# A layer kernel whose last four token tiles are transposed in 32x32 blocks on VectorE, by way of DRAM, and whose first weight rows are loaded one by one

## The chip, the cores and the metric

The kernel runs on one core of one Trainium2 chip. The metric is the device time of one execution in microseconds (us). Other work does not share the core. The engines are TensorE (PE in the profile; its weight loads are PEld), VectorE (DVE), ScalarE (ACT), GpSimd (POOL) and SyncE (SP). SP computes nothing here: it is the queue on which nearly all DMA transfers are issued, in the order of the program.

## The reference

The input `x` has 2048 tokens of 512 numbers. After a layer norm, two branches read the same normalized rows, and the output is `x + s * g`:

```python
xn = _layernorm(x, axis=-1)
s = _A_ref(xn, A_wqkv, A_w_phi, A_wo)                 # linear attention, 32 heads of 16
g = _silu(_B_ref(xn, B_W_gate, B_W_up, B_W_down))     # gated ReLU unit, 1376 wide
return x + s * g
...
qkv = (x @ wqkv) ...                                  # q, k, v
phi_k = concat(softmax(k @ w_phi), softmax(-(k @ w_phi)))       # and phi_q alike
o = phi_q (phi_k^T v) / (phi_q (phi_k^T 1) + 1e-6);  s = o @ wo
h = relu(x @ W_gate) * (x @ W_up);  g = silu(h @ W_down)
```

Everything is float32. The kernel keeps that precision by splitting each operand into a high part and a low part (`split`, L193) and making each product from three matmuls (`mm3`, L198).

## The kernel before, in words

**Stage 1, tokens.** The 2048 tokens are 16 tiles of 128 rows, and the loop `for n in range(N)` (L1046) takes one tile in each turn. Loads, norms and transposes run ahead of it: a turn `n` loads tile n+7 (`load_x`), takes the sums of tile n+6 on ScalarE (`norm_stats`), the inverse root of tile n+5 on VectorE and GpSimd (`norm_scale`), applies the norm of tile n+4 on ScalarE (`norm_apply`), and transposes tile n+3 (`turn`, LEAD = 3). `turn` (L320) is four TensorE transposes of 128x128 into one PSUM bank, `pxT` (`transpose_x`); then ScalarE writes the high part into the SBUF tensor `XT` (`hi_xt`) and a full copy `xf` (`full_xt`), and VectorE writes the low part (`lo_xt`), both from PSUM. From each two neighbouring tiles GpSimd makes four sums and differences (`sums_x`, into new tiles `sa` and `sb`), which `sums_hi` (ScalarE) and `sums_lo` (GpSimd) split into `XT` too. For the first eight tiles most of `XT` is spilled to DRAM and read back for the second half of stage 2.

In the same turn TensorE projects tile n to keys (`pk`, 12 matmuls of 512 columns) and values (`pv`, 12), one of sixteen query pieces (`pq`, 12), and adds phi^T v of an earlier tile to four PSUM banks that stay occupied through the stage (`pkv`, 8 matmuls of 256 columns). VectorE makes the exponents from `pk` (two reductions, two subtractions), later the low part of v, the sums, a reciprocal that it writes into the bank of `pv`, and the scaled features `ek`. The pool of PSUM banks has 8; with four held by `pkv`, four go round.

**Stage 2, gated unit and queries.** For each half of the tokens and each of 11 slices of the hidden width, `gate_up` makes seven products (`pa` to `pd`) and `down` adds rows of `py`. Beside that runs the query side (`all_queries`, `q_pair`): VectorE turns the stored query pieces back in 32x32 blocks, finds bounds, ScalarE exponentiates, and so on. Between `state()` (L1119), which builds the attention state, and the first query pair of the first half stands `yield 24,` (L1176).

**What sets the order.** Instructions keep the order of the program on each engine. That order comes from a planner, the class `Clock` (L62): it counts columns of TensorE work (`now`; a matmul of 512 columns adds 542), estimates when each tile will be ready (a DMA 8000 after its issue), and at every `pump()` releases the next step of generators whose wants are met: for the wants "sync" and "tensor" 3000 counts after the estimate, for an engine when its backlog is under a limit. `yield k,` waits k times 512 counts. Nothing of this exists at run time; there, each engine waits for semaphores, in order.

**Start.** Before the loop, the weights of keys, queries and values are loaded on SP in the order written in L960 to L991, folded on TensorE (`fold`) and split; `wv_hi` and `wv_lo` (L977, L980) split the value rows k = 0 to 3 on ScalarE and GpSimd.

Of the kernel before, what the change touches and what calls it, by code (L numbers as in the profile page):

```python
# [1 line left out]

# [5 lines left out]
F32 = mybir.dt.float32  # L8
F32R = mybir.dt.float32r
AF = mybir.ActivationFunctionType  # L10
# [28 lines left out]
START = (12, 15)  # L39
WO_WITH = (4, 5, 6, 7)  # L40

A21, A22, A11, A12, S1, S2, S3, S4 = range(8)


class InOrder:
# [16 lines left out]
class Clock:  # L62
# [4 lines left out]
    LIMIT = {"vector": 2000, "scalar": 2000, "gpsimd": 2500}  # L67
    MARGIN = 3000
    LANDING, ISSUE = 8000, 1500
    shared = None  # L70

    def __init__(self):
        self.free = dict.fromkeys(self.FIXED, 0.0)
# [10 lines left out]
    def issued(self, key, name, a, k):  # L84
        o, ins = a[0], [*a[1:], *k.values()]
        n = max(x.free_size() for x in [o, *ins] if hasattr(x, "free_size"))
        start = max([self.now, *(self.there(x) + 200 for x in ins)])
        if name == "dma_start":
            self.ready[o.name] = start + self.LANDING
            if key == "gpsimd":  # L90
                self.free[key] = max(start, self.free[key]) + self.ISSUE
            return
        cost = self.RATE[key] * n
        if key == "tensor":
            n = o.free_size()
# [6 lines left out]
        self.ready[o.name] = self.free[key] + (380 if key == "tensor" else 0)  # L102

    def add(self, gen, after=0, limit=1, first=False):
        self.work.insert(0 if first else len(self.work), [self.now + after * BT, (None,), gen, limit])
# [53 lines left out]
def layer_kernel(ctx: ExitStack, tc: tile.TileContext, x, wkT, wqT, wv, wo, wf, cst, out):  # L159
# [24 lines left out]
    def f32(t):  # L184
        return t.bitcast(F32)

    def add(engine, o, a, b, op=ALU.add):
        engine.tensor_tensor(o, a, b, op=op)
# [62 lines left out]
        return lambda: split(*map(by_parity, w[k]), even_first(p))  # L251


    mhalf = sb.tile([P, 96], F32, name="mhalf")[:, 0:1]
    XT = sb.tile([P, 8, 2, 2, BT], F32R, tag="XT", name="XT")
    pace.shared = XT.name
    XN, XF, SF = {}, {}, {}

    def norm_stats(n):
        xt = X.pop(n)  # L260
        xn = u2((P, D), "xn")
        sm, ss, rs, bias = small(1, "lm"), small(1, "lv"), small(1, "lr"), small(1, "lb")
        nc.scalar.activation(xn, xt, AF.Copy, scale=-1.0 / D, accum_out=sm)
        nc.scalar.activation(xn, xt, AF.Square, bias=sm, accum_out=ss)
        XN[n] = xn, xt, bias, rs, sm, ss

    def norm_scale(n):
        xn, xt, bias, rs, sm, ss = XN[n]
        nc.vector.tensor_scalar(rs, ss, 1.0 / D, 1e-5, op0=ALU.mult, op1=ALU.add)
        nc.gpsimd.tensor_tensor(rs, rs, mhalf, op=ALU.pow)  # L270

    def norm_apply(n):
        xn, xt, bias, rs, sm, ss = XN[n]
        nc.vector.tensor_scalar(bias, sm, rs, None, op0=ALU.mult)
        nc.scalar.activation(xn, xt, AF.Identity, bias=bias, scale=rs)
        XN[n] = xn

    def norm_vector(n):

# [14 lines left out]
    def cols(n):  # L294
        i = order[n][1]
        return slice(i * P, (i + 1) * P)
# [8 lines left out]
    def xt_part(n, s):  # L305

        a = A21 if n % 2 else A11
        return XT[:, a:a + 2, s, :, cols(n)]

    def hi_xt(n, p):  # L310
        nc.scalar.activation(xt_part(n, 0), p, AF.Copy)

    def full_xt(n, p):
        XF[n] = u2((P, 2, 2, P), "xf")
        nc.scalar.activation(XF[n], p, AF.Copy)

    def lo_xt(n, p):
        add(nc.vector, xt_part(n, 1), p, f32(xt_part(n, 0)), ALU.subtract)

    def turn(m, full=True):  # L320
        p = transpose_x(m)
# [5 lines left out]
    def sums_x(n):  # L327

        x0, x1 = XF.pop(n - 1), XF.pop(n)
        sa, sb_ = u2((P, 2, 2, P), "sa"), u2((P, 2, 2, P), "sb")  # L330
        add(nc.gpsimd, sa[:, 0], x1[:, 0], x1[:, 1])
        add(nc.gpsimd, sb_[:, 0], x0[:, 0], x1[:, 0], ALU.subtract)
        add(nc.gpsimd, sa[:, 1], sa[:, 0], x0[:, 0], ALU.subtract)
        add(nc.gpsimd, sb_[:, 1], x0[:, 1], sa[:, 1], ALU.subtract)
        SF[n] = sa, sb_

    def sums_hi(n):
        for s, c in zip(SF[n], (S1, S3)):
            nc.scalar.activation(XT[:, c:c + 2, 0, :, cols(n)], s, AF.Copy)

    def sums_lo(n):
        for s, c in zip(SF.pop(n), (S1, S3)):
            add(nc.gpsimd, XT[:, c:c + 2, 1, :, cols(n)], s, f32(XT[:, c:c + 2, 0, :, cols(n)]), ALU.subtract)

    def xt_cols(n):
        a, c = A21 if n % 2 else A11, cols(n)
# [107 lines left out]
    DONE = set()  # L454

    def f_load(f):
        if f == AHEAD[-1]:

            t = u4((P, 2, 2, 2, P), "rawg")
            RAW[f] = [t[:, c] for c in range(2)], u2((P, D), "rawd")  # L460
            nc.sync.dma_start(t.rearrange("p c k s f -> p (c k s f)"), wf[f][:, :1024])
        else:
            RAW[f] = two("rawg", f not in AHEAD), u2((P, D), "rawd")
            for c in range(2):
                nc.sync.dma_start(RAW[f][0][c].rearrange("p k s f -> p (k s f)"), wf[f][:, c * 512:(c + 1) * 512])
        nc.sync.dma_start(RAW[f][1], wf[f][:, 1024:])

    def w_pair(name):
# [556 lines left out]
    folds[1]()  # L1025
    norm_vector_apply(3)

    def all_preps():
# [16 lines left out]
    at = [0]  # L1045
# [287 lines left out]
```

## Time and profile before

| | us |
|---|---|
| three runs | 562.86, 564.63, 564.69 (median 564.63) |
| profiled execution, device time | 562.9 |
| its span, first to last instruction | 561.1 |
| outside the span | 1.8 |
| mean granted TensorE clock | 0.999 |

The span is read on the timeline of the engines. Stage 1 turns take 8.7 to 9.8 us each and end at 166.9 us; the first half of stage 2 ends at about 355 us with the last `pso` matmuls, and the second half takes the rest. In the views, tile names stand for the operands, L58 is the line of the helper through which every instruction is recorded, and times are from the start of the span. In the chain of waits each row is start, length and group.

### The profile page before, as it was taken

Reading aid. Unit: us, or ns where it says so; the run is one execution under the profiler, and the core shown is the slowest. Engines: PE = TensorE matmul, PEld = TensorE weight load, DVE = VectorE, ACT = ScalarE, POOL = GpSimd, SP = SyncE. Lnnn points to the kernel's source line nnn. Section 1 sums busy time; section 2 is a strip of 40 time slices with the busy share of each in tenths; the row PEclk is TensorE's granted clock in tenths of the full one; section 3 lists DMA queues with packets and bytes.
Section 4 is the critical chain, followed back from the end, with each engine's and each line's share of the span. In section 5 each row is a group of like instructions: output and inputs, shape, how many; then the busy total and the mean of one; then the engine's idle time right before and its main releaser. Section 6 shows DMA issues by size and latency. Waiting matters only on the chain.

```text
span 561.1 us, 8204 instructions
## 1 busy us (share of the span) xinstructions
PE 556.3 (99%) x2618; PEld 466.0 (83%) x2618; DVE 412.0 (73%) x623; ACT 282.7 (50%) x504; POOL 416.2 (74%) x356
## 2 busy tenths in 40 slices
PE   9999999999999999999999999999999999999997
PEld 8888888888888888888888888888888888888886
DVE  5978777677656898999798432699995959775324
ACT  3898687765545456444425251234463544534500
POOL 1689987898888386998889242572879788888474
PEclk9999999999999999999999999999999999999999
DMA  8349999765599827979767899997475666659675
GB/s 282 136 150 245 274 277 330 213 167 166 150 297 314 327 77 276 326 270 324 263 240 230 246 356 419 401 374 282 137 225 178 219 204 206 207 166 284 170 237 193
DMA packets 84538, 137.98 MB, mean 246 GB/s; under 512 B 7824, under 2 KB 34320, under 8 KB 83600
## 3 DMA queue, kind: packets, MB, share of 16 engines
q1 hardware_dynamic: 81040, 125.33, 65.1%
q0 software_dynamic: 3312, 12.06, 11.0%
q8 instruction: 21, 0.34, 0.3%
q14 instruction: 21, 0.17, 0.1%
q10 hardware_dynamic: 144, 0.07, 0.0%
HBM read 76.87 MB, written 52.69 MB: 231 GB/s over the span
## 4 chain that ended last, share of the span: by engine, by line
PE 99%; DVE 0%; issue 0%
PE py L58 21%; PE pc L58 11%; PE pa L58 11%; PE pd L58 11%; PE pv L58 8%; PE pk L58 8%; PE pq L58 8%; PE pso L58 8%; PE pb L58 5%; PE pkv L58 3%; PE pnum L58 3%; PE pxT L58 1%; PE pfold L58 1%; PE pidle L58 1%; PE pz L58 0%; DVE yk L58 0%
## 5 line engine op out<-in xcount | busy, mean ns | idle before, releaser
L58 PE MATMUL py<-fdh,hl 128*128 128x512 f32 x176 | 68.5, 389 | 0.0
L58 PE MATMUL py<-fdh,hh 128*128 128x512 f32 x176 | 68.5, 389 | 0.0
L58 PE MATMUL py<-fdl,hh 128*128 128x512 f32 x176 | 68.5, 389 | 0.0
L58 PE MATMUL pa<-XT,wa 128*128 128x512 f32 x264 | 67.4, 389 | 0.0
L58 POOL TENSOR_TENSOR hl<-e,hh 128x512 fp32r<-128x512 f32 x22 | 28.5, 1296 | 44.9 <-ACT hh L58 40.0
L58 PEld LDWEIGHTS pa<-XT,wa 128*128 128x128 f32 x264 | 49.5, 188 | 10.2
L58 ACT ACTIVATE hh<-e 128x512 fp32r<-128x512 f32 x22 | 13.9, 633 | 72.5 <-DVE e L58 70.1
L58 DVE TENSOR_TENSOR y<-py,y 128x512 f32<-128x512 f32 x40 | 27.5, 689 | 24.7 <-PE py L58 24.7
L58 POOL TENSOR_TENSOR phl<-ek,phl 128x1024 fp32r<-128x1024 f32 x15 | 36.1, 2409 | 11.1 <-ACT phl L58 11.1
L58 PE MATMUL pv<-wvh,XT 128*128 128x512 f32 x128 | 43.5, 401 | 0.0
L58 PE MATMUL pk<-wkh,XT 128*128 128x512 f32 x128 | 42.4, 392 | 0.0
L58 POOL TENSOR_TENSOR hl<-u,hh 128x512 fp32r<-128x512 f32 x22 | 28.8, 1311 | 16.6 <-ACT hh L58 14.3
L58 POOL TENSOR_TENSOR ez<-eq,zB 128x1024 f32<-128x1024 f32 x16 | 38.5, 2411 | 3.3 <-ACT eq L58 2.7
L58 PE MATMUL pq<-XT,wqh 128*128 128x512 f32 (+1 forms) x144 | 40.3, 366 | 0.0
L58 PEld LDWEIGHTS py<-fdh,hl 128*128 128x128 f32 x176 | 33.0, 188 | 6.9
L58 PEld LDWEIGHTS py<-fdh,hh 128*128 128x128 f32 x176 | 33.0, 188 | 6.8
L58 PEld LDWEIGHTS py<-fdl,hh 128*128 128x128 f32 x176 | 33.0, 188 | 6.8
L58 POOL TENSOR_TENSOR ol<-of,oh 128x512 fp32r<-128x512 f32 (+1 forms) x13 | 19.9, 1551 | 23.3 <-ACT oh L58 15.9
L58 PE MATMUL pc<-XT,wc 128*128 128x512 f32 x132 | 34.9, 392 | 0.0
L58 PE MATMUL pd<-XT,wc 128*128 128x512 f32 x132 | 33.8, 389 | 0.0
L58 PE MATMUL pc<-XT,wb 128*128 128x512 f32 x132 | 33.7, 389 | 0.0
L58 PE MATMUL pd<-XT,wd 128*128 128x512 f32 x132 | 33.5, 389 | 0.0
(162 smaller groups left out, 1581.0 us busy)
## 6 DMA issues: line engine op xcount, KB each, us to landing
zacc<-ek POOLq DMA_DIRECT2D x15, 512.0 KB, 6.0
xts<-XT SPq DMA_DIRECT2D x4, 1792.0 KB, 8.8
XT<-xts SPq DMA_DIRECT2D x7, 1024.0 KB, 19.6
wa<-ws SPq DMA_DIRECT2D x26, 256.0 KB, 5.0
wb<-ws SPq DMA_DIRECT2D x26, 256.0 KB, 4.4
wc<-ws SPq DMA_DIRECT2D x26, 256.0 KB, 5.0
ws<-wa SPq DMA_DIRECT2D x22, 256.0 KB, 4.5
ws<-wb SPq DMA_DIRECT2D x22, 256.0 KB, 4.2
```

Source lines behind the costliest of these rows:

```text
L58: return self.tc.keep_in_program_order(op(*a, **k))
```

## The change

Four things are changed.

1. Tiles 12 to 15 (`BLOCKWISE = 12`) are no longer transposed on TensorE. `norm_apply` writes them with columns regrouped, and a generator `by_blocks` stores the tile to DRAM, loads it back in four transfers that spread 32-row blocks over the partitions (runs of 128 numbers, 512 bytes), transposes it on VectorE in 32x32 blocks, and makes the high and low parts from the result in SBUF, without a PSUM bank and without the full copy. (`pace.mark("scalar")` is a name that stands for the planner's present estimate of ScalarE; `hi_xt` and `lo_xt` regroup their views of `XT` to the blocks.) Loads, sums, scales and norms of the last tiles are drawn one turn ahead (`up_to`).
2. `sums_x` works in place in `xf`, for all tiles; the order of the combinations in `XT` changes to match.
3. At the start, value rows 0 to 3 and query rows 2 and 3 are loaded in a transfer each, instead of two rows in one; the second prefetched gate slice is loaded in two transfers instead of one.
4. The `yield 24,` before the first query pair is gone.

```diff
-A21, A22, A11, A12, S1, S2, S3, S4 = range(8)
+A21, A22, A11, A12, S3, S1, S2, S4 = range(8)
+BLOCKWISE = 12
+LAND = (12, 12)
...
     def norm_apply(n):
...
+        if n < BLOCKWISE:
+            nc.scalar.activation(xn, xt, AF.Identity, bias=bias, scale=rs)
+        else:
+            nc.scalar.activation(xn.rearrange("p (a k i) -> p k a i", a=4, i=32),
+                                 xt.rearrange("p (k a i) -> p k a i", a=4, i=32), AF.Identity, bias=bias, scale=rs)
+            TURN[n] = pace.add(by_blocks(n, xn), 0, 3, True)
+
+    def by_blocks(n, xn):
+        xd = dram((P, D), f"xn{n}")
+        yield "sync", xn
+        nc.sync.dma_start(xd, xn)
+        yield LAND[0],
+        yield "sync", xd
+        t = u2((P, 4, P), "xp")
+        for a in range(4):
+            r = slice(32 * a, 32 * a + 32)
+            nc.sync.dma_start(t[r], xd.rearrange("(b q) (a c) -> a q b c", q=32, a=4)[a])
+        yield LAND[1],
+        yield "sync", t
+        while at[0] < n - LEAD:
+            yield 1,
+        yield "vector", t
+        o = u2((P, D), "xf")
+        nc.vector.transpose(o, t.rearrange("p b c -> p (b c)"))
+        XF[n] = o.rearrange("p (b c k q) -> p c k b q", b=4, c=2, k=2)
+        yield "scalar", o
+        hi_xt(n, XF[n])
+        yield "vector", pace.mark("scalar")
+        lo_xt(n, XF[n])
+        if n % 2:
+            yield "gpsimd", o
+            sums_x(n)
...
     def sums_x(n):
-        sa, sb_ = u2((P, 2, 2, P), "sa"), u2((P, 2, 2, P), "sb")
-        add(nc.gpsimd, sa[:, 0], x1[:, 0], x1[:, 1])
...
+        add(nc.gpsimd, x1[:, 1], x1[:, 0], x1[:, 1])
+        add(nc.gpsimd, x1[:, 0], x0[:, 0], x1[:, 0], ALU.subtract)
+        add(nc.gpsimd, x0[:, 0], x1[:, 1], x0[:, 0], ALU.subtract)
+        add(nc.gpsimd, x0[:, 1], x0[:, 1], x0[:, 0], ALU.subtract)
...
-    nc.sync.dma_start(wv_raw[:, 0:2, :], wv[:, 0:2, :])
-    nc.sync.dma_start(wq_raw[:, 2:4, :], wqT[:, 2:4, :])
+    for k in range(2):
+        nc.sync.dma_start(wv_raw[:, k, :], wv[:, k, :])
+    for k in range(2, 4):
+        nc.sync.dma_start(wq_raw[:, k, :], wqT[:, k, :])
     load_x(2)
-    nc.sync.dma_start(wv_raw[:, 2:4, :], wv[:, 2:4, :])
+    for k in range(2, 4):
+        nc.sync.dma_start(wv_raw[:, k, :], wv[:, k, :])
...
-        if n + 7 < N:
-            load_x(n + 7)
+        up_to(n + 7 + (n > 6), load_x)
...
-        if 1 < n < N - 4:
-            norm_apply(n + 4)
-        if 0 < n < N - 5:
-            norm_scale(n + 5)
+        if n > 1:
+            up_to(n + 4 + (n > 9), norm_apply)
+        if n:
+            up_to(n + 5 + (n > 8), norm_scale)
...
-        turned = [turn(n + LEAD)] if 1 < n < N - LEAD else [turn(3)] if n == 1 else []
+        if 1 < n < N - LEAD and m >= BLOCKWISE:
+            turned = []
+        else:
+            turned = [turn(m)] if 1 < n < N - LEAD else [turn(3)] if n == 1 else []
...
-        if n + 6 < N:
-            norm_stats(n + 6)
+        up_to(n + 6 + (n > 7), norm_stats)
         if n % 2 and n + 2 < N:
+            for m in (n + 1, n + 2):
+                if m in TURN:
+                    pace.finish(TURN.pop(m))
             sums_hi(n + 2)
...
             yield from state()
-            yield 24,
```

More of the change, by code (lines that the diff above doesn't have):

```diff
@@ L1 @@
 from contextlib import ExitStack
+from types import SimpleNamespace
 import concourse.bass as bass
@@ L69 @@
     LANDING, ISSUE = 8000, 1500
-    shared = None
+    shared, marks = None, 0
     def __init__(self):
@@ L102, in issued, with mark @@
         self.ready[o.name] = self.free[key] + (380 if key == "tensor" else 0)
+    def mark(self, key):
+        self.marks += 1
+        t = SimpleNamespace(name=f"mark{self.marks}")
+        self.ready[t.name] = self.free[key]
+        return t
     def add(self, gen, after=0, limit=1, first=False):
@@ L251, in fold @@
         return lambda: split(*map(by_parity, w[k]), even_first(p))
-    mhalf = sb.tile([P, 96], F32, name="mhalf")[:, 0:1]
+    mhalf = sb.tile([P, 96], F32, name="mhalf")
+    mhalf, eps = mhalf[:, 0:1], mhalf[:, 1:2]
     XT = sb.tile([P, 8, 2, 2, BT], F32R, tag="XT", name="XT")
     pace.shared = XT.name
-    XN, XF, SF = {}, {}, {}
+    XN, XF, SF, TURN, at = {}, {}, {}, {}, [0]
     def norm_stats(n):
@@ L261, in norm_stats @@
         xn = u2((P, D), "xn")
+        unread = xn or ps(name="unread")
         sm, ss, rs, bias = small(1, "lm"), small(1, "lv"), small(1, "lr"), small(1, "lb")
-        nc.scalar.activation(xn, xt, AF.Copy, scale=-1.0 / D, accum_out=sm)
-        nc.scalar.activation(xn, xt, AF.Square, bias=sm, accum_out=ss)
-        XN[n] = xn, xt, bias, rs, sm, ss
+        nc.scalar.activation(unread, xt, AF.Copy, scale=-1.0 / D, accum_out=sm)
+        nc.scalar.activation(unread, xt, AF.Square, bias=sm, accum_out=ss)
+        XN[n] = xt, bias, rs, sm, ss, xn
     def norm_scale(n):
-        xn, xt, bias, rs, sm, ss = XN[n]
+        xt, bias, rs, sm, ss, xn = XN[n]
         nc.vector.tensor_scalar(rs, ss, 1.0 / D, 1e-5, op0=ALU.mult, op1=ALU.add)
@@ L272, in norm_apply @@
     def norm_apply(n):
-        xn, xt, bias, rs, sm, ss = XN[n]
+        xt, bias, rs, sm, ss, xn = XN[n]
         nc.vector.tensor_scalar(bias, sm, rs, None, op0=ALU.mult)
-        nc.scalar.activation(xn, xt, AF.Identity, bias=bias, scale=rs)
-        XN[n] = xn
+        xn = xn or u2((P, D), "xn")
+        if n < BLOCKWISE:
+            nc.scalar.activation(xn, xt, AF.Identity, bias=bias, scale=rs)
+            XN[n] = xn
+        else:
[27 more added lines that the diff above has]
+            sums_x(n)
     def norm_vector(n):
@@ L308, in xt_part, with like @@
         return XT[:, a:a + 2, s, :, cols(n)]
+    def like(t, p):
+        return t.rearrange("p c k (b q) -> p c k b q", q=32) if len(p.shape) == 5 else t
     def hi_xt(n, p):
-        nc.scalar.activation(xt_part(n, 0), p, AF.Copy)
+        nc.scalar.activation(like(xt_part(n, 0), p), p, AF.Copy)
     def full_xt(n, p):
@@ L317, in lo_xt @@
     def lo_xt(n, p):
-        add(nc.vector, xt_part(n, 1), p, f32(xt_part(n, 0)), ALU.subtract)
+        add(nc.vector, like(xt_part(n, 1), p), p, f32(like(xt_part(n, 0), p)), ALU.subtract)
     def turn(m, full=True):
@@ L329, in sums_x @@
         x0, x1 = XF.pop(n - 1), XF.pop(n)
-        sa, sb_ = u2((P, 2, 2, P), "sa"), u2((P, 2, 2, P), "sb")
-        add(nc.gpsimd, sa[:, 0], x1[:, 0], x1[:, 1])
[L332 to L335, printed above, removed]
+        add(nc.gpsimd, x1[:, 1], x1[:, 0], x1[:, 1])
+        add(nc.gpsimd, x1[:, 0], x0[:, 0], x1[:, 0], ALU.subtract)
+        add(nc.gpsimd, x0[:, 0], x1[:, 1], x0[:, 0], ALU.subtract)
+        add(nc.gpsimd, x0[:, 1], x0[:, 1], x0[:, 0], ALU.subtract)
+        SF[n] = x1, x0
     def sums_hi(n):
-        for s, c in zip(SF[n], (S1, S3)):
-            nc.scalar.activation(XT[:, c:c + 2, 0, :, cols(n)], s, AF.Copy)
+        for s, c in zip(SF[n], (S3, S2)):
+            nc.scalar.activation(like(XT[:, c:c + 2, 0, :, cols(n)], s), s, AF.Copy)
     def sums_lo(n):
-        for s, c in zip(SF.pop(n), (S1, S3)):
-            add(nc.gpsimd, XT[:, c:c + 2, 1, :, cols(n)], s, f32(XT[:, c:c + 2, 0, :, cols(n)]), ALU.subtract)
+        for s, c in zip(SF.pop(n), (S3, S2)):
+            add(nc.gpsimd, like(XT[:, c:c + 2, 1, :, cols(n)], s), s, f32(like(XT[:, c:c + 2, 0, :, cols(n)], s)),
+                ALU.subtract)
     def xt_cols(n):
@@ L456, in f_load @@
     def f_load(f):
[L457 to L465, printed above, removed]
+        RAW[f] = two("rawg", f not in AHEAD), u2((P, D), "rawd")
+        for c in range(2):
+            nc.sync.dma_start(RAW[f][0][c].rearrange("p k s f -> p (k s f)"), wf[f][:, c * 512:(c + 1) * 512])
         nc.sync.dma_start(RAW[f][1], wf[f][:, 1024:])
@@ L1026, in layer_kernel, with up_to @@
     norm_vector_apply(3)
+    done = {norm_scale: 5, norm_apply: 5, norm_stats: 5, load_x: 6}
+    def up_to(m, op):
+        for i in range(done[op] + 1, min(m, N - 1) + 1):
+            op(i)
+            done[op] = i
     def all_preps():
@@ L1060, in layer_kernel @@
             pace.pump()
-        turned = [turn(n + LEAD)] if 1 < n < N - LEAD else [turn(3)] if n == 1 else []
+        m = n + LEAD
+        if 1 < n < N - LEAD and m >= BLOCKWISE:
+            turned = []
+        else:
+            turned = [turn(m)] if 1 < n < N - LEAD else [turn(3)] if n == 1 else []
         pace.pump()
```

1 line of the change is left out of this document (removed).

## The prediction, made before the result was seen

> **What bounds the kernel now.** I read the page's busy shares first, then the waits of TensorE, then the windows, because a share alone does not say whether an engine waits.
>
> ```profile
> PE 556.3 (99%) x2618; PEld 466.0 (83%) x2618; DVE 412.0 (73%) x623; ACT 282.7 (50%) x504; POOL 416.2 (74%) x356
> ```
> ```profile
> PE pidle L58 <- DVE mhalf L58: 1.1, 1, 1.1
> ```
> ```profile
> 0.00:10.00 10.00, 8.94 (x54) 8.78 (x55) 3.82 (x11) 3.30 (x5) 0.77 (x5) 1.00 0.79 245
> 520.00:561.00 41.00, 37.40 (x181) 31.43 (x179) 13.51 (x20) 9.50 (x18) 23.17 (x19) 0.99 0.66 200
> ```
>
> The second fence is the whole list of waits of TensorE: one, of 1.1 us, at the start. The windows (columns: PE, PEld, DVE, ACT, POOL, clock, DMA share, GB/s) show where the 4.8 us that are not PE lie: 1.06 before its first instruction and 3.6 after its last. Between them TensorE has work without a break, at full clock. So time goes only when TensorE has fewer instructions, and is lost only when something makes it wait. All else in the change counts through that second door. The bound for "no change" is 0.5% either way, 2.8 us, about what a measurement of this kernel can tell from none.
>
> **Part 1, the transposes removed.** The chain of waits in order of time shows one turn with a transposed tile and one without:
>
> ```profile
> 115.69 2.72 PE pk L58 x12
> 118.41 0.95 PE pkv L58 x8
> 119.36 0.44 PE pxT L58 x4
> 119.80 2.76 PE pv L58 x12
> 122.55 2.72 PE pq L58 x12
> ...
> 134.86 2.72 PE pk L58 x12
> 137.58 0.95 PE pkv L58 x8
> 138.53 2.75 PE pv L58 x12
> 141.28 2.72 PE pq L58 x12
> ```
> ```profile
> 115.69:125.27 9.58, 9.58 (x49) 8.14 (x49) 8.02 (x12) 5.49 (x9) 9.50 (x10) 1.00 0.74 201
> 125.27:134.86 9.59, 9.59 (x50) 8.15 (x49) 6.72 (x10) 5.39 (x9) 9.11 (x9) 1.00 0.81 210
> 134.86:144.00 9.14, 9.14 (x45) 7.71 (x45) 6.13 (x9) 4.65 (x8) 8.01 (x10) 1.00 0.45 117
> ```
>
> The same pk, pkv, pv and pq stand in both; the turn is 9.59 with four pxT and 9.14 without, 0.45 us. Four tiles (12 to 15, in turns 9 to 12): 4 x 0.45 = **1.8 us off the bound**. That is the only TensorE work that changes.
>
> **Part 2, what the new path adds, and where it lies.**
>
> ```profile
> L58 DVE STREAM_TRANSPOSE pq<-pql 128x512 f32<-128x512 f32 x16 | 11.3, 704 | 0.0
> L58 DVE TENSOR_TENSOR XT<-pxT,XT 128x512 fp32r<-128x512 f32 x16 | 11.0, 690 | 6.9 <-ACT xf L58 5.4 <-ACT XT L58 1.5
> L58 DVE TENSOR_TENSOR yk<-yk,sx 128x512 f32<-128x512 f32 x1 | 1.3, 1254 | 0.0
> ```
> ```profile
> L58 ACT ACTIVATE xf<-pxT 128x512 f32<-128x512 f32 x16 | 9.4, 588 | 0.0
> ```
>
> VectorE gains four block transposes of this very shape, 4 x 0.70 = 2.8 us. Its low part now has both operands in SBUF: 0.69 if that is free, 1.25 by the one row of that kind, so 0 to 0.56 more per tile. Together 0.7 to 1.3 us per turn, on a busy time of 6.7 and 8.0 in the two turns quoted: under 9.3 even in the fuller one, whose neighbours have room. ScalarE loses the full copy, 0.59 per tile. GpSimd does the same sums, in place. None of this is on TensorE, so it is costed at nothing; the cover is the slack below.
>
> The Trainium skill, "SBUF — State Buffer", section "SBUF: two separate sides", says that a VectorE instruction with two SBUF inputs and a GpSimd one that reads SBUF exclude each other for a whole instruction. The 1254 ns against 690 agree with it; by that rule each low part could also hold a GpSimd instruction up, and the four of them would cost VectorE 2.2 us, still off TensorE.
>
> The wait added is VectorE's: the transpose stands in its queue until the four loads have landed. Behind it stand the exponents of the turn, the features, and so the release of the PSUM banks.
>
> ```profile
> 91.21 0.80 ACT L58 ACTIVATE xn<-xt,lb,lr 128x512 f32<-128x512 f32 x1
> 99.43 0.80 ACT L58 ACTIVATE xn<-xt,lb,lr 128x512 f32<-128x512 f32 x1
> 111.78 0.80 ACT L58 ACTIVATE xn<-xt,lb,lr 128x512 f32<-128x512 f32 x1
> ```
> ```profile
> 87.81 2.75 PE pk L58 x12
> ...
> 106.10 2.72 PE pk L58 x12
> ```
> ```profile
> 117.34 1.22 DVE L58 TENSOR_TENSOR ek<-ek,pv 128x1024 f32<-128x1024 f32 x1
> ```
> ```profile
> 110.14 0.41 SPq L58 DMA_DIRECT2D ws<-wa  x1
> 110.64 0.41 SPq L58 DMA_DIRECT2D ws<-wb  x1
> ```
> ```profile
> pq<-pqs SPq DMA_DIRECT2D x12, 128.0 KB, 2.8
> ws<-wd SPq DMA_DIRECT2D x1, 256.0 KB, 2.8
> ```
> ```profile
> xt<-x SPq DMA_DIRECT2D x16, 256.0 KB, 7.3
> ```
>
> Tiles 12, 13 and 14 are normed at 91.2, 99.4 and 111.8 (turns 8, 9, 10). After that come the store, four issues of 0.41, and the landing of the loads. From the landings between 88 and 140 us: 2.8 + 1.6 + 2.8 = 7.2 us; from the median of the x loads (most of them in the crowded start): 7.3 + 1.6 + 7.3 = 16.2. I take 7.2, since those rows are of the same stage and queue, and keep 16.2 for the range. The planner lets the transpose into VectorE's queue about 10.5 us after the start of the turn in which the tile is normed: 3000 counts of margin, then twice 8000 + 3000, and 542 counts are one matmul of 2.72/12 = 0.227 us, so 1.3 + 2 x 4.6. The turns start with pk; for tile 12 that is 87.8 + 10.5 = 98.3, for tile 14 106.1 + 10.5 = 116.6, where VectorE is busy with turn 10's features (ek, to 118.6). Data are there at 92.0 + 7.2 = 99.2 and 112.6 + 7.2 = 119.8. So VectorE stands 1 to 2 us per tile, less for 13, nothing for 15, which must wait for turn 12 anyway. The twenty extra SP issues (4 tiles x 5 x 0.41 = 8 us over 40) and 2 MB move nothing that TensorE reads in this stage.
>
> The slack: four banks go round, and without pxT a turn asks for three. The last reader of turn 10's pv is the ek above; it ends at 118.6, and its bank is next asked for at turn 11's pq, 122.1 without the transposes: 3.5 us, against one request earlier (119.8) before. A stand of 1 to 2 us is hidden; I put 0.3 us into the sum for small losses.
>
> **Part 3, start and queries.**
>
> ```profile
> 16.05 1.15 ACT L58 ACTIVATE wvh<-wvr 128x512 fp32r<-128x512 f32 x2
> 16.75 2.56 POOL L58 TENSOR_TENSOR wvl<-wvr,wvh 128x512 fp32r<-128x512 f32 x2 [1.01 <-ACT wvh L58]
> ```
> ```profile
> 17.50 2.76 PE pv L58 x12
> ```
>
> TensorE has no wait at the start, so single rows cannot gain anything. They can lose: the low part of the last value row ends at 19.31, and the last of the four groups of pv begins at 17.50 + 3/4 x 2.76 = 19.6. Cover 0.3 us. But ScalarE starts on rows 2 and 3 without waiting for a DMA, so the three extra issues (3 x 0.41 = 1.2 us on SP) must first eat the time by which the rows are early. Value 0, bounds 0 and +0.9 (1.2 less the cover).
>
> ```profile
> 186.53 0.72 DVE L58 STREAM_TRANSPOSE pq<-pql 128x512 f32<-128x512 f32 x1
> ```
> ```profile
> 180.00:195.00 15.00, 15.00 (x68) 12.43 (x67) 11.96 (x20) 7.14 (x15) 7.58 (x5) 1.00 0.93 344
> 195.00:210.00 15.00, 15.00 (x68) 12.43 (x67) 14.83 (x22) 7.57 (x14) 11.12 (x11) 1.00 0.22 80
> ```
>
> `yield 24,` is 24 x 512 counts, 5.1 us: the first query pair moves from 186.5 to about 181.4, into a window where VectorE has 3 us free. TensorE stayed at 15.00 of 15 even where VectorE was at 14.83, so I cost this at 0, bounds -0.5 and +1. The in-place sums and the split gate load: 0.
>
> **Sum.** -1.8 + 0.3 = -1.5 us: 562.9 becomes 561.4. The median of the three runs is 1.7 above the profiled execution, and the four times stand at two levels, 562.9 and 564.6; from the upper one the same step gives 563.1. I predict 562.3, between, 0.3% down on either.
>
> **Rivals.**
>
> *The gain comes back as waits* (562.3 + 1.8, about 564). Several small losses of the bounds above, a late bank here, a late row there, add up to the 1.8. For it: GpSimd at 9.50 of 9.58 in turn 11, so whatever blocks it shifts the low parts. Against: features are used three turns later.
>
> *VectorE waits for DRAM and TensorE for VectorE* (slower). Place: turns 9 to 11, at the new transpose. It decides where store, issues and loads take more than about 9.5 us: tile 14's data must be there by 118.6 + 3.5 of slack, from 112.6. Each us beyond that is a us of TensorE, for tiles 12, 13 and 14. Halfway between the two prices (11.7 us), 3 x 2.2 = 6.6 us less the 1.8: 567.7; at 16.2, 3 x 6.7 - 1.8 = 18.3, about 581. For it: two trips in a row on a queue in order, whose x loads had a median of 7.3. Against: landings of 2.8 in the stage itself.
>
> *VectorE as the bound.* The Trainium skill, "VectorE: DVE Perf Modes", section "Rules for kernel authors", sends a 128x128 transpose to TensorE where PSUM will do, and keeps VectorE for 32x32 blocks. In rows: VectorE pays 0.70 plus up to 0.56 where TensorE paid 0.45. It would bind if its turn passed 9.14; 6.7 + 1.3 and 8.0 + 1.3 say that one turn could, by 0.2 us, and the next takes it back. As a rival: +0.2 to +1, so about 562.5, inside the forecast's range.
>
> *More than the transposes goes.* An earlier query side or free banks remove waits too. No wait of TensorE but the first is listed, so at most fractions: 559.8, and only then faster by over 0.5%.
>
> **Chances.** Forecast with the VectorE rival 0.50; gain given back 0.15 (564); DRAM wait 0.23; more gone 0.12. Faster by over 0.5%: 0.12. Within: 0.50 + 0.15 = 0.65. Slower: 0.23. The range runs from 560.0, the lower level less 2.9, to 567.5, the upper level 564.6 and 2.9 of net stalls, leaving out the greater part of the DRAM rival (0.15) and a little below (0.04).
>
> **What would show it.** Right: no pxT after tile 11, turns 9 to 12 shorter by 0.45 each, the list of TensorE's waits as short as now; the new transposes at 0.70 with an idle time before them, released by a DMA, of 1 to 2 us; their low parts between 0.69 and 1.25. Wrong: waits of pq or pv on VectorE in turns 10 to 12; landings of the four loads over 5 us; a pv at the start that waits for GpSimd; a later first query transpose than 182.

## The result, and the profile after

| | before | after |
|---|---|---|
| median of six runs each, us | 563.64 (562.48 to 564.69) | 568.41 (566.97 to 569.43) |
| profiled execution, us | 562.9 | 568.9 |
| its span, us | 561.1 | 567.1 |
| mean granted TensorE clock | 0.999 | 0.994 |

The changed kernel is slower: 1.0082 times the time before, 95% interval 1.0061 to 1.0103. That is 4.8 us by the medians and 6.0 by the two profiled spans, outside the forecast's range.

The busy shares on the page of the changed kernel, then the whole list of TensorE's waits:

```profile
PE 557.0 (98%) x2602; PEld 466.1 (82%) x2602; DVE 424.6 (75%) x627; ACT 280.4 (49%) x500; POOL 417.2 (74%) x356
```
```profile
PE pv L63 <- DVE ek L63: 5.4, 1, 5.4
PE pidle L63 <- DVE mhalf L63: 1.1, 1, 1.1
```

TensorE has its sixteen transposes less (2602 for 2618), yet is busy for 0.7 us more, and one wait of 5.4 us is new: a pv on VectorE's `ek`. VectorE's busy time went from 412.0 to 424.6, so 12.6 us more. To see where it ends, take the first and the last start of gate product `pa`, one row of the tile view of each kernel, before and then after:

```profile
L58 PE MATMUL pa<-XT,wa x264: 389/389/398, 166.8 to 511.0; 128*128 128x512 f32 x132
```
```profile
L63 PE MATMUL pa<-XT,wa x264: 389/389/398, 172.9 to 517.1; 128*128 128x512 f32 x132
```

Stage 2 begins 6.1 us later and ends 6.1 us later. All of the loss is in stage 1. There the chain of waits in order of time shows the place:

```profile
133.09 6.49 DVE XT L63 x2
139.58 0.66 DVE mx L63 x2
...
141.30 0.68 DVE ek L63
141.98 0.14 issue
142.12 5.25 PE pv L63 x12
```

In the chain before, only TensorE stood here. Now VectorE works for 6.5 us on two low parts, then on the exponents of turn 12, and only when the last `ek` has read the `pk` bank of that turn may the pv of turn 13 write to it. This pv then takes 5.25 us, where the same twelve matmuls took 2.75. The windows (columns: PE, PEld, DVE, ACT, POOL, clock, DMA share, GB/s) show the granted clock beside it:

```profile
135.00:140.00 5.00, 1.75 (x12) 1.43 (x10) 5.00 (x3) 0.00 (x0) 4.92 (x5) 1.00 0.53 105
140.00:145.00 5.00, 2.88 (x7) 2.33 (x8) 4.35 (x7) 2.12 (x4) 1.60 (x3) 0.52 0.09 30
145.00:150.00 5.00, 5.00 (x20) 3.98 (x19) 4.41 (x7) 2.70 (x4) 2.55 (x2) 0.80 0.53 184
```

While TensorE stands, VectorE and GpSimd are both full. Afterwards the granted clock is 0.52, then 0.80. The account is -1.8 (transposes) + 5.4 (wait) + 2.5 (pv at the low clock, 5.25 less 2.75) = +6.1, against the 6.1 of stage 1.

Why are two low parts so long? The groups of VectorE, shapes apart:

```profile
L63 DVE TENSOR_TENSOR XT<-xf,XT 128x512 fp32r<-128x512 f32 x4 | 12.4, 3134 | 0.5 <-ACT XT L63 0.5
...
L63 DVE TENSOR_TENSOR XT<-pxT,XT 128x512 fp32r<-128x512 f32 x12 | 8.3, 689 | 5.0 <-ACT xf L63 3.4 <-ACT XT L63 1.5
L63 DVE STREAM_TRANSPOSE xf<-xp 128x512 f32<-128x512 f32 x4 | 2.7, 696 | 0.0
```

The low part from PSUM still takes 689 ns; the same subtraction with both operands in SBUF takes 3134. The block transposes take what was forecast, with no idle time before them. Set the four low parts, from VectorE's timeline in narrow windows, beside GpSimd's timeline:

```profile
118.83 3.74 DVE L63 TENSOR_TENSOR XT<-xf,XT 128x512 fp32r<-128x512 f32 x1
...
122.50 2.23 DVE L63 TENSOR_TENSOR XT<-xf,XT 128x512 fp32r<-128x512 f32 x1
...
133.09 2.47 DVE L63 TENSOR_TENSOR XT<-xf,XT 128x512 fp32r<-128x512 f32 x1 [0.48 <-ACT XT L63]
...
135.48 4.10 DVE L63 TENSOR_TENSOR XT<-xf,XT 128x512 fp32r<-128x512 f32 x1
```
```profile
119.52 2.49 POOL L63 TENSOR_TENSOR phl<-ek,phl 128x1024 fp32r<-128x1024 f32 x1
...
122.46 1.71 POOL L63 TENSOR_TENSOR wc<-tab,wc 128x512 fp32r<-128x512 f32 x1
...
132.61 2.39 POOL L63 TENSOR_TENSOR phl<-ek,phl 128x1024 fp32r<-128x1024 f32 x1 [4.61 <-ACT phl L63]
...
135.55 2.79 POOL L63 TENSOR_TENSOR XT<-xf,XT 128x512 fp32r<-128x512 f32 x2
138.01 1.00 POOL L63 TENSOR_TENSOR xf<-xf 128x256 f32<-128x256 f32 x1
```

Add start and length. The low parts end at 122.57, 124.73, 135.56 and 139.58; GpSimd instructions end at 122.01, 124.17, 135.00 and 139.01. Each low part ends 0.56 us after a GpSimd instruction ends. The last one began in a gap at 135.48 and yet waited out three of them, two `XT` and one `xf`, which follow each other without a pause (the last row is the first `xf` alone, from a narrow window).

The store and the four loads through DRAM, in the view of DMA issues (KB each, median us to landing), land a little later than the forecast put them (2.8 each):

```profile
xn<-xn SPq DMA_DIRECT2D x4, 256.0 KB, 3.4
xp<-xn SPq DMA_DIRECT2D x16, 64.0 KB, 3.1
```

My theory after this reading, T: a VectorE subtraction with two SBUF operands cannot go on while GpSimd runs; in this stage GpSimd hardly pauses; so each low part of a block tile costs about 2.4 us more on VectorE, the exponents behind it release their bank too late, TensorE stands, and its clock falls. Rival A: the regrouped views that these low parts read and write are slow by themselves. Rival B: the source is harmless, it is the planner's placing (two block tiles beside each other, with transposes and low parts ahead of the exponents) that makes VectorE late. Rival C: the other parts of the change (in-place sums, single loads at the start, no pause) cost the time.

### The profile page after: what moved, and what is told of

Read it like the earlier page. It is cut to its first block, busy times and chain, and to the rows that moved or that the text cites. A ratio compares the mean times of both kernels' runs of the same rounds, so it can differ in the third digit from the quotient of the medians.

```text
span 567.1 us, 8212 instructions
## 1 busy us (share of the span) xinstructions
PE 557.0 (98%) x2602; PEld 466.1 (82%) x2602; DVE 424.6 (75%) x627; ACT 280.4 (49%) x500; POOL 417.2 (74%) x356
## 4 chain that ended last, share of the span: by engine, by line
PE 74%; DVE 3%; ACT 0%; issue 0%; ACTq 0%
PE py L63 21%; PE pc L63 11%; PE pd L63 11%; PE pa L63 11%; PE pso L63 8%; PE pb L63 5%; PE pnum L63 3%; PE pq L63 2%; PE pv L63 2%; DVE XT L63 1%; PE pk L63 1%; PE pkv L63 1%; DVE ek L63 0%; DVE mx L63 0%; DVE sm L63 0%
## 5 line engine op out<-in xcount | busy, mean ns | idle before, releaser
L63 PE MATMUL pv<-wvh,XT 128*128 128x512 f32 x128 | 44.8, 412 | 5.4 <-DVE ek L63 5.4
L63 PEld LDWEIGHTS pv<-wvh,XT 128*128 128x128 f32 x128 | 25.2, 197 | 10.7 <-issue 5.5
```

Of the source, the lines that this page charges most:

```text
L63: return self.tc.keep_in_program_order(op(*a, **k))
```

## The experiments

Ratios are to the kernel before, run on the same chip, with 95% intervals. A span is that of the profiled execution.

### e1_psum: the source moved to PSUM

The block transposes go to a PSUM bank; high and low part read it there, and ScalarE makes the full copy for the sums again (`v` is the regrouped view of `po`). The views and the planner's rules stay; the order that they give does not quite, as shown below.

```diff
-        o = u2((P, D), "xf")
-        nc.vector.transpose(o, t.rearrange("p b c -> p (b c)"))
+        o, po = u2((P, D), "xf"), ps((P, D), name="pxB")
+        nc.vector.transpose(po, t.rearrange("p b c -> p (b c)"))
...
-        hi_xt(n, XF[n])
+        hi_xt(n, v)
+        nc.scalar.activation(o, po, AF.Copy)
         yield "vector", pace.mark("scalar")
-        lo_xt(n, XF[n])
+        lo_xt(n, v)
```

> The changed kernel, with the block transpose written to a PSUM bank, both parts read from there and a full copy made by ScalarE for the sums. Theory (the low part stands behind GpSimd because both its operands are in SBUF): its four low parts fall from 3.13 us to 0.7 us, TensorE has no wait at a pv, the clock stays at 1.00, and the time falls from 568.4 to about 561.5 to 563, that is 0.3% under the kernel before. Rival A (the block access pattern of 32 numbers is slow on VectorE): the low parts stay near 3 us and the time near 568, since the pattern is the same. Rival B (two transposes in a row ahead of the exponents are what hurts, not their length): the wait stays, smaller, 2 to 4 us.

Measured: 564.21, ratio 1.0010 (1.0001 to 1.0019), span 562.5 against 567.1 after. The low parts' group, and the waits of TensorE in the turns of stage 1 (two more, of 0.8 and 0.3 us, come before the turns with block tiles, at the start):

```profile
L63 DVE TENSOR_TENSOR XT<-pxB,XT 128x512 fp32r<-128x512 f32 x4 | 2.6, 680 | 0.9 <-ACT xf L63 0.9
```
```profile
PE pk L63 <- ACT pqs L63: 0.7, 1, 0.7
PE pq L63 <- DVE ek L63: 0.6, 1, 0.6
PE pv L63 <- DVE ek L63: 0.3, 1, 0.3
```

The views are the same, and the low part takes 680 ns for 3134: rival A falls. The span is 4.6 us shorter, of the 6.0 that were lost, but that is not the source alone, since the planner's order moved with it. In the changed kernel the low parts of tiles 14 and 15 (133.09 and 135.48) stand ahead of the exponents of turn 12; here exponents and features of that turn go first:

```profile
128.31 1.31 DVE L63 STREAM_TRANSPOSE pxB<-xp 128x512 f32<-128x512 f32 x2
129.53 1.25 DVE L63 TENSOR_REDUCE mx<-pk 128x32 f32<-128x512 f32 x2
...
136.15 1.28 DVE L63 TENSOR_TENSOR XT<-pxB,XT 128x512 fp32r<-128x512 f32 x2
```

So source and placing are told apart only where VectorE's order is the same, in e4_lo_pool and between e10_spaced and e11_spaced_sbuf. What stays in the turns is 1.6 us of small waits, perhaps because two block tiles now each hold a bank at once; with one tile per turn, in e10_spaced, they are gone.

### e2_rest: the change without the block path

```diff
-BLOCKWISE = 12
+BLOCKWISE = 16
```

> The changed kernel with BLOCKWISE at 16, so that all tiles are transposed on TensorE again: start loads, in-place sums, earlier norms and the missing pause remain. Theory: none of these touches the bound, 562.5 to 564.7, the same as before within 0.3%, no wait of TensorE but the first. Rival C (part of the 6 us comes from the rest of the change): above 565.

Measured: 564.11, ratio 1.0008 (0.9998 to 1.0018), span 562.7, no wait of TensorE in the turns of stage 1 (0.9 us for a weight load before them). Rival C falls: in-place sums, single rows, early norms and the missing pause together are no more than 0.2%.

### e3_lo_sbuf: the source in the kernel before

TensorE's transposes stay; only the low parts of tiles 12 to 15 read the full copy in SBUF, in the plain order of columns (and the sums leave the copy in place for them).

```diff
-        add(nc.vector, xt_part(n, 1), p, f32(xt_part(n, 0)), ALU.subtract)
+        add(nc.vector, xt_part(n, 1), XF[n] if n >= 12 else p, f32(xt_part(n, 0)), ALU.subtract)
```

> The kernel before with a single edit: the low parts of tiles 12 to 15 read the full copy in SBUF in place of the PSUM bank; the tiles are still transposed on TensorE and the pattern has runs of 128 numbers. Theory: these four low parts take 2 to 4 us each in place of 0.69, in the turns where GpSimd is full; as they come one per turn, TensorE may wait by 0 to 4 us, 563 to 568. Rival A (pattern): they stay at 0.69 and the time does not move.

Measured: 563.94, ratio 1.0008 (0.9999 to 1.0017), no wait of TensorE in the turns of stage 1. The group, then the longest low part on VectorE's timeline, then GpSimd's instruction beside it:

```profile
L58 DVE TENSOR_TENSOR XT<-xf,XT 128x512 fp32r<-128x512 f32 x4 | 6.5, 1618 | 1.8 <-ACT xf L58 1.8
```
```profile
122.88 2.68 DVE L58 TENSOR_TENSOR XT<-xf,XT 128x512 fp32r<-128x512 f32 x1 [0.34 <-ACT xf L58]
```
```profile
122.60 2.41 POOL L58 TENSOR_TENSOR phl<-ek,phl 128x1024 fp32r<-128x1024 f32 x1
```

122.88 + 2.68 is 125.56, and 122.60 + 2.41 is 125.01: again 0.55 us after GpSimd's end, here with neither blocks nor DRAM. The four took 0.89, 1.03, 1.88 and 2.68 us, by where they fell against GpSimd. Spread one to a turn and behind the exponents, 4 x 0.93 us more on VectorE is hidden: the penalty alone does not slow the kernel.

The end of this trace also has the comparison that no run was made for, the same subtraction of half the width with GpSimd beside it and without. VectorE's two, then the last GpSimd instruction of the program:

```profile
556.59 0.96 DVE L58 TENSOR_TENSOR yk<-yk,sx 128x256 f32<-128x256 f32 x1
...
558.03 0.42 DVE L58 TENSOR_TENSOR yk<-yk,sx 128x256 f32<-128x256 f32 x1
```
```profile
555.54 1.74 POOL L58 TENSOR_TENSOR y<-y,sx 128x512 f32<-128x512 f32 x1
```

The first ends at 557.55, 0.27 us after GpSimd's 557.28; the second, with no GpSimd instruction beside it, takes 0.42.

### e4_lo_pool: the low parts on GpSimd

```diff
-        add(nc.vector, like(xt_part(n, 1), p), p, f32(like(xt_part(n, 0), p)), ALU.subtract)
+        add(nc.gpsimd if n >= BLOCKWISE else nc.vector, like(xt_part(n, 1), p), p, f32(like(xt_part(n, 0), p)), ALU.subtract)
...
-        yield "vector", pace.mark("scalar")
+        yield "gpsimd", pace.mark("scalar")
```

(The sums of a pair also wait in the planner for both low parts.)

> The changed kernel with the low parts of the four block tiles on GpSimd in place of VectorE. Theory: on GpSimd they take about 1.55 us like its other low parts, VectorE is free of them, exponents are not late and the 5.4 us wait at pv is gone; GpSimd gains 6 us over four turns and may push the features' low parts out: 561.5 to 565. Rival B (the transposes in the queue are what hurts): a wait of TensorE on VectorE remains.

Measured: 568.65, ratio 1.0094 (1.0080 to 1.0108). My expectation was wrong. Stage 1 has no wait, as forecast, but the list of TensorE's waits has

```profile
PE pa L63 <- POOL wa L63: 5.1, 1, 5.1
```

The four low parts take 1.55 us each on GpSimd, some 6 us, and GpSimd also prepares stage 2's weights: `wa` was late by 5.1. I had counted its busy share, not what stood last in its queue. Behind that wait the granted clock was 0.50 for the next 5 us, and from the first to the last `pa` passed 347.2 us, where it was 344.2 before. The run does show that VectorE's low parts make the wait in stage 1: all else on VectorE keeps the order of the changed kernel, the two block transposes ahead of the exponents included, and without the low parts the wait is gone. Rival B as it stood for this run, the transposes in the queue, falls.

### e5_warm and e5b_warm: TensorE kept busy in its wait

The changed kernel with 22 products of a zero matrix, added into the `pkv` banks while the pv of turn 13 waits; in e5b_warm the planner does not count them, so that the order stays.

```diff
+        if n == 13:
+            for i in range(22):
+                nc.tensor.matmul(PKV[i % 4].rearrange("p a b -> p (a b)"), zz, WK[0][0], start=False, stop=False,
+                                 skip_group_check=True)
         pv = project(n, WV, "pv")
```

> The changed kernel with 22 products of a zero tile added into the pkv banks (they add zero) just ahead of pv in turn 13, where TensorE waits 5.4 us and then runs its 12 matmuls in 5.25 us in place of 2.75. Theory (the idle time itself lowers the granted clock for the next few us, so the wait is paid twice): the 22 matmuls take 5.0 us inside the wait, the clock stays at 1.00, pv takes 2.75 again, and the time falls by about 2.5 us, to 566. Rival (the slow pv has another cause, or the clock falls anyway): the time stays at 568.4 or grows.

Measured: 569.61, ratio 1.0101 (1.0074 to 1.0127). Counting the products moved later work (a new wait of pb on GpSimd, 0.9 us), so it settles nothing on the total; hence the second form.

> e5_warm again, with the 22 zero products kept out of the planner's count, so that all other instructions keep the order of the changed kernel. In e5_warm pv ran at 2.75 us again behind the zero products, but the planner had shifted stage 2. Theory (the clock falls because TensorE stood idle): stage 1 and the whole are about 2.4 us shorter than the changed kernel, 566. Rival: no change, 568.4.

Measured: 568.63, ratio 1.0101 (1.0079 to 1.0123), span 566.3. Its windows, for the stretch quoted of the changed kernel:

```profile
140.00:145.00 5.00, 5.00 (x24) 4.14 (x23) 4.34 (x6) 2.21 (x5) 0.07 (x1) 1.00 0.35 112
145.00:150.00 5.00, 5.00 (x26) 4.22 (x25) 4.34 (x8) 3.80 (x7) 4.28 (x4) 1.00 0.39 124
```

The clock stays at 1.00, and stage 1 ends at 169.7 instead of 172.9; 0.8 us of that lie ahead of this pv, which starts at 141.31, and the rest in it. So the low clock follows from the idle time and costs about 2.5 us there. The Trainium skill, "TensorE: Matmul & The Clock Gate", section "HAM oscillation — how this bites in real kernels", warns of idle gaps over some 3.4 us; the 5.4 us here agree, as do the 5.1 of e4_lo_pool and the 3.8 of e8_blocks8 below, and gaps of 1.2 us and less at full clock (e11_spaced_sbuf, e1_psum) left it at 1.00. In the total the gain isn't shown: the last `pa` starts 2.0 us earlier (515.1), but the profiled span has only 0.8 us less, and the median nothing.

### e9_lo_turn, e8_blocks8: one block tile per turn, from PSUM

From e1_psum: loads, norms and start as before the change, so that one tile is ready per turn; its low part is placed after the exponents, where the others are; the pause is back. In e8_blocks8 tiles 8 to 15 go that way.

```diff
-        up_to(n + 4 + (n > 9), norm_apply)
+        up_to(n + 4, norm_apply)
...
-        yield "vector", pace.mark("scalar")
-        lo_xt(n, v)
+        LOS.append((n, v))
...
-            features(n, ..., lambda: [lo_xt(*t) for t in turned])
+            features(n, ..., lambda: [[lo_xt(*t) for t in turned], low_parts()])
...
             yield from state()
+            yield 24,
```

> The kernel with block transposes into PSUM, and in addition: start loads, pause before the queries and the turns of loads and norms as in the kernel before, and each low part put where turn's own low part stood, so that each turn has one block transpose and one low part. Theory (what is left of the loss in the PSUM version are banks held by two transposes at once, 1.6 us, and the start): no wait of TensorE in stage 1, 1.8 us less work, 561.6 to 562 against 563.4, ratio 0.9965 to 0.9975. Rival (the gain of 1.8 is taken back somewhere else whatever the order): ratio 1.000.

Measured: 580.33, ratio 1.0299 (1.0277 to 1.0321). The tile view of `pa`, and TensorE's longest wait:

```profile
L63 PE MATMUL pa<-XT,wa x264: 389/389/628, 165.0 to 528.4; 128*128 128x512 f32 x132
```
```profile
PE pnum L63 <- ACT pTh L63: 11.9, 4, 9.3
```

Stage 1 ends at 165.0, 1.8 us before the kernel before, just the four transposes. Then the second stage loses far more: up to 318.9 us TensorE stands 9.3 us for the query side, whose last `peT` of the first half comes at 324.8, against 305.2 before. Between the first and the last `pa` lie 363.4 us for 344.2 before; 11.9 of the 19.2 more are waits, and the granted clock was 0.50 behind the longest of them, from 318.9 to 332.8.

> As e9_lo_turn with BLOCKWISE at 8: eight tiles by blocks. Theory: the gain scales with the tiles, 8 x 0.45 = 3.6 us, 559.8 to 560.5, ratio 0.9935 to 0.995, as long as VectorE's 0.7 us more per turn and the added DMAs fit; in turns 5 to 8 GpSimd and the queues are fuller, so a wait of 1 to 2 us would not surprise. Rival: the trips through DRAM are late in those turns and TensorE waits, above 563.

Measured: 568.74, ratio 1.0099 (1.0073 to 1.0124). With eight tiles stage 1 waits again (3.8 us of a pk on `ek`, 1.8 us of pq on low parts), and the group of block transposes says what stands behind it:

```profile
L63 DVE STREAM_TRANSPOSE pxB<-xp 128x512 f32<-128x512 f32 x8 | 5.8, 726 | 14.3 <-DMA xp<-xn 14.0 <-issue 0.3
```

VectorE waits 14.0 us for the loads from DRAM. The longest of these waits, 7.6 us, ends with the transpose at 97.81; the exponents follow it, and TensorE's 3.8 us end behind them at 101.04, with a granted clock of 0.50 over the next 3 us. An issue of an x load had held SP from 84.48 to 90.40, and the four loads were issued after it; the landings have medians of 5.1 (store) and 4.3 us (loads). So the recorded rival came true here: the gain doesn't scale, because in the earlier turns the trips through DRAM are late.

### e10_spaced: the same without the pause

```diff
             yield from state()
-            yield 24,
```

> As e9_lo_turn (block transposes into PSUM, one transpose and one low part per turn, start loads and norms as in the kernel before), but without the pause before the queries. e9_lo_turn ended stage 1 at 165.0 us, 1.8 earlier than before, and lost 15 us in stage 2 to waits of pnum on ScalarE's copies for the queries. Theory (the pause that suits the old order of stage 2 makes the query side late in the new one): no such waits, 561.6 to 562, ratio 0.9965 to 0.9975. Rival (the earlier end of stage 1 itself upsets stage 2): the waits of pnum stay, 570 or more.

Measured: 561.51, ratio **0.9970 (0.9959 to 0.9981)**, faster than both kernels. Waits, low parts and `pa`:

```profile
PE pidle L63 <- DVE mhalf L63: 1.1, 1, 1.1
PE pv L63 <- POOL wvl L63: 0.2, 1, 0.2
```
```profile
L63 DVE TENSOR_TENSOR XT<-pxB,XT 128x512 fp32r<-128x512 f32 x4 | 2.7, 682 | 0.0
```
```profile
L63 PE MATMUL pa<-XT,wa x264: 388/389/397, 165.3 to 509.5; 128*128 128x512 f32 x132
```

Stage 2 starts and ends 1.5 us earlier than before (165.3 and 509.5, against 166.8 and 511.0). It differs from e9_lo_turn by one line, and by 19 us: the pause changed the planner's order of the whole query side, at the profiled executions' first query transpose from 184.2 to 190.9 us.

### e11_spaced_sbuf: the same spacing, operands in SBUF

```diff
-        o, po = u2((P, D), "xf"), ps((P, D), name="pxB")
-        nc.vector.transpose(po, t.rearrange("p b c -> p (b c)"))
+        o = u2((P, D), "xf")
+        nc.vector.transpose(o, t.rearrange("p b c -> p (b c)"))
```

(High and low part read `o`; the copy is gone; the sums wait in the planner for both low parts.)

> As e10_spaced, but the block transposes go to SBUF and the low parts read SBUF, as in the changed kernel: only the spacing (one transpose and one low part per turn) differs from it on VectorE. Theory (the length of the low parts behind GpSimd is what hurts): they still take 1.5 to 4 us each; one per turn leaves VectorE at 8 to 10 us of 9.14, so some wait of TensorE remains, 1 to 4 us, 562.5 to 566. Rival (two transposes and two low parts in one turn are what hurts): no wait, 561.6.

Measured: 564.56 (562.83 to 567.41), ratio 1.0023 (1.0009 to 1.0037); e10_spaced, run beside it on the same chip, is 3.05 us below. The longest low part, GpSimd beside it, and TensorE's waits:

```profile
119.86 4.93 DVE L63 TENSOR_TENSOR XT<-xf,XT 128x512 fp32r<-128x512 f32 x1
```
```profile
118.73 2.63 POOL L63 TENSOR_TENSOR phl<-ek,phl 128x1024 fp32r<-128x1024 f32 x1
...
121.71 1.83 POOL L63 TENSOR_TENSOR wc<-tab,wc 128x512 fp32r<-128x512 f32 x1
122.96 1.27 POOL L63 TENSOR_TENSOR wd<-rawg,wd 128x256 fp32r<-128x256 f32 x1
```
```profile
PE pb L63 <- POOL wb L63: 1.2, 1, 1.2
...
PE pq L63 <- DVE XT L63: 0.9, 1, 0.9
```

One tile per turn, and still one low part of 4.93 us: it ends at 124.79, 0.56 after the last of a row of GpSimd instructions (124.23). The first of them, `phl`, ends at 121.36, and `wc` starts 0.35 us later: the low part did not get in there. In the changed kernel the gap between the same two was 0.45 (122.01 to 122.46), and it did; but it also got in at 139.01, where the next `xf` starts 0.08 us later. So the gap alone does not decide. The others took 1.04, 1.28 and 1.42. So placing (with the start loads as before) takes back about 3.4 of the 4.8 us, each kernel's median set against the kernel before on its own chip, but not the gain. The source is worth another 3, here at the same order on VectorE; a part of it is the 1.2 us wait of pb for GpSimd's `wb`, whose place in GpSimd's order moved too.

### e7_start and e12_nopause: two small parts of the change alone

```diff
-    nc.sync.dma_start(wv_raw[:, 0:2, :], wv[:, 0:2, :])
+    for k in range(2):
+        nc.sync.dma_start(wv_raw[:, k, :], wv[:, k, :])
...
```

> The kernel before with the start loads of the changed one alone. As predicted: 0 to +0.9 us. The rest of the change together measured +0.08%; if the start carries that, this gives +0.3 to +0.8 us (ratio 1.0005 to 1.0015) with a wait of pv on the last value row's low part; if not, 1.000.

Measured: 563.87, ratio 1.0010 (0.9996 to 1.0023), with pv waiting for the low value rows 0.5 us in the profile.

```diff
             yield from state()
-            yield 24,
```

> The kernel before without the pause before the query pairs, nothing else. As predicted: 0, bounds -0.5 and +1 us (ratio 0.999 to 1.002), the first query transpose near 181.5. Rival (stage 2 hangs on this pause): waits of TensorE in stage 2 of several us.

Measured: 564.05, ratio 1.0015 (1.0006 to 1.0024); the first query transpose moved from 186.5 to 181.2, no new wait in stage 2. Both are small, on the side of a loss; the interval of e7_start includes none.

## Why the prediction was wrong, point by point

**The step that failed** is the low part with both operands in SBUF, "0.69 if that is free, 1.25 by the one row of that kind, so 0 to 0.56 more per tile". It was 2.44 more (3134 less 690), 4 x 2.44 = 9.8 us on VectorE where I had allowed 2.2 at most. By the timelines of the trace before, the 1254 ns row ran from 555.30 to 556.55, beside a GpSimd subtraction that ended at 556.00. So its 0.56 us over 0.69 were the rest of one GpSimd instruction, not a price; the stage of the change has GpSimd at 9.5 of 9.6 us per turn, a number that I quoted for a rival and not for this price. Another row of the trace before, which I passed over, warns that the 1254 is no constant: the same operation of half the width takes 426 ns with two SBUF operands and 418 with one of them in PSUM:

```profile
L58 DVE TENSOR_TENSOR yk<-yk,sx 128x256 f32<-128x256 f32 x2 | 0.9, 426 | 0.1
L58 DVE TENSOR_TENSOR yk<-pso,yk 128x256 f32<-128x256 f32 x2 | 0.8, 418 | 0.1
```

Both of the first kind ran after GpSimd's last instruction. The pair says "free when GpSimd lets it through", so the price is how long GpSimd doesn't. The rule of the Trainium skill ("SBUF — State Buffer", section "SBUF: two separate sides") pointed to the right pair of engines. I took "a whole instruction" as the most that VectorE could lose; here it lost up to three in a row, while GpSimd lost 0.5 us at most: `phl` beside low parts took 2.49 and 2.39 us in the changed kernel, 2.40 to 2.43 in the kernel before. The longest is 2.94, in e5b_warm; the 2.63 in e11_spaced_sbuf stands in e10_spaced too, whose low part reads PSUM.

**The slack** of 3.5 us was worked out for the bank of pv and its features. The late one was the bank of pk, read by the exponents, which stood behind two transposes and two low parts. By the timelines, the exponents of turn 12 ended at 130.5 before and at 142.0 after, 11.5 us later. TensorE asked for that bank at 136.7 (142.1 less the wait): a slack of 6.2 us, larger than mine, and 11.5 - 6.2 = 5.3, the wait. That the low parts of the four block tiles came in two clumps is the planner's doing: it reckons a low part at 160 counts and 2.4 a column, 1389 counts or 0.58 us, and norms drawn a turn ahead let tiles 14 and 15 through together. I had followed one tile at a time, and placed it wrongly: tile 12's transpose, forecast at 98.3 to 99.2, came at 110.15. It took both, the length and the clump: in the clumped order without low parts on VectorE there was no wait (e4_lo_pool), and spaced out the same long low parts made one of 0.9 (e11_spaced_sbuf). The low parts from PSUM in the clumped order were not run. An estimate from this timeline: two low parts of 0.69 in place of the 6.49 us would have ended the exponents of turn 12 about 5.1 us earlier, at 136.9, and left a wait of 0.2.

**The price of a wait.** I priced a us of wait at a us. A wait of 5.4 us cost 2.5 more in clock within stage 1 (shown by e5b_warm for the stage, not for the total). The waits of 5.1 in e4_lo_pool and 3.8 in e8_blocks8 had a granted clock of 0.50 behind them as well.

**What held.** The transposes are worth 1.8 us on TensorE: stage 1 of e9_lo_turn ends 1.8 earlier, and e10_spaced as a whole runs 1.7 faster by the medians. The landings of the DRAM path held, 3.4 and 3.1; the four issues did not, which took 5.4 us for tile 12 (SP, 96.53 to 101.90) where I put 1.6. That trip took about 12 us, longer than the 9.5 at which I had let it bind, and still VectorE never waited for it (idle 0.0), as the transposes came later than forecast. So with four tiles the slower rival that I named was the wrong one: the wait of TensorE on VectorE that I took for its sign came, in turn 13 and from another mechanism. With eight tiles, in e8_blocks8, it was the right one. The block transpose takes 0.70. Start and pause, measured apart, lie within their bounds, at about +0.8 each by the medians where I took 0; the first query transpose moved as forecast in e12_nopause (181.2), but in the changed kernel, with stage 1 late by 6.1 and another order, it came at 191.7; e2_rest, which has both, is 0.5 to 0.7 above before, so the two don't seem to add.

**Open.** Why the pause of e9_lo_turn makes the query side so late was not followed beyond the order. Whether the start rows or something else set the waits of 0.2 to 0.9 us before the first turn can't be told: they come and go with either start, e10_spaced with the old one included. That the low parts wait for GpSimd is read from three things: all twenty of them with two SBUF operands in the kept traces (the changed kernel, e3, e5, e5b, e11) end 0.54 to 0.57 us after a GpSimd instruction does; from PSUM, in e1_psum and e10_spaced, they take 0.68; and at the end of the trace of e3 the same kind of subtraction is held beside GpSimd and not without it. No run took GpSimd's work away beside the low parts themselves.

## What to carry to other kernels

Where GpSimd is full at that place, price a VectorE instruction with two SBUF operands by several GpSimd instructions in a row (here up to three), not by its own length, and try one operand in PSUM (here 0.68 us for 1.04 to 4.93 at the same order). Before counting a gain on the bounding engine, ask of each helper what stands behind the new instruction in its queue and which bank that holds, for all the tiles that come together. When a hand-made or planned order moves with the edit, test the edit and the order apart: here the source gave 3 us at one order, and one pause 19.

## What was not expected of the hardware

- An instruction of 0.69 us was held for 4.10 and 4.93 us while GpSimd instructions followed each other with 0.35 us between them or less (which of these gaps lets it in stays open); every quoted one ended 0.55 to 0.57 us after a GpSimd instruction did. A subtraction of half the width took 0.96 us beside GpSimd and 0.42 without it, in one trace (e3_lo_sbuf).
- The same low part took 0.89 to 1.42 us in five of the eight cases of e3_lo_sbuf and e11_spaced_sbuf, where the GpSimd instruction beside it was near its end; these too ended 0.54 to 0.56 us after it.
- After 5.4 us without work on TensorE the granted clock was 0.52, then 0.80 in the windows that follow (140 to 145 and 145 to 150 us); with zero products in the gap it stayed at 1.00. After 3.8 us (e8_blocks8) and 5.1 us (e4_lo_pool) it was 0.50 over the next 3 and 5 us.
